# Attention over PSUM in three pairs and a bank: other places for the scores and the row maxima from step 112 on

## The chip, the cores and the metric

The kernel runs on one core of one Trainium2 chip. The metric is the device time of one execution in microseconds (us); three runs were made. The core has five engines that work side by side, each in the order of its own instructions: TensorE (PE, with its weight loads shown apart as PEld), VectorE (DVE), ScalarE (ACT), GpSimd (POOL) and SyncE (SP). Matmul results land in PSUM, which this kernel divides into eight banks of 512 fp32 per partition.

## The reference

A transformer block with modulation from a conditioning vector: layer norm, attention with 16 heads of width 28 over 2048 tokens, then layer norms and an MLP. Dimensions: S = 2048, D = 448, F = 1792.

```python
mod = (silu(c) @ w_mod).reshape(1, 6, 1, D)          # sa, ca, ga, sb, cb, gb
h = layernorm(x) * (1 + ca) + sa
q, k, v = split_heads(h @ wqkv)                      # 16 heads of 28
p = softmax((q @ k.T) * 28 ** -0.5)                  # 2048 x 2048 for each head
x = x + ga * ((p @ v) @ wo)
h = layernorm(x) * (1 + cb) + sb
x = x + gb * (gelu(layernorm(h) @ w1 + b1) @ w2 + b2)
```

## The kernel before

Three phases follow each other. Phase 1 (to 182 us) makes q, k and v, phase 2 (182 to 846 us) is the attention, phase 3 (to the end) the MLP. The order of each engine's instructions is the order in which the Python code issues them; nothing reorders them. Between engines semaphores are set, and they follow from tiles: an instruction waits until the earlier instructions that read or write its tile, or the tile that had the same place, are done.

Heads are taken in four groups `g` of four, queries in four blocks `qt` of 512. A pair (g, qt) is a unit `u` (0 to 15), and a unit has 16 steps `kt`, one for each 128 keys, so phase 2 has 256 steps. In step s of unit u PE computes the transposed scores of 128 keys and 512 queries for the four heads. Each head has 32 rows of the array, so up to four of its matmuls run side by side. The scores come in two halves (`hf`): heads 0 and 1, then heads 2 and 3. A half is a tile of two banks made by six matmuls (three terms of a split product, two heads). ACT takes the exponential of a half in one instruction (128 x 1024), and four matmuls, later called the AV block, multiply the exponentials of the step before with v into the bank `o`. They use all 128 rows and 32 columns each.

The softmax needs its row maximum. It is computed for later units in advance: `max_one` makes a block of scores with queries along partitions (one matmul on 32 rows, 512 keys) in a bank, and DVE reduces the bank to one column. Such a matmul with its reduction is called a maximum here. The queue `mxq` holds them, `emit_max(n, half)` issues the next ones, for heads of the asked half where it finds one, and `finish_max` issues what is still missing for a unit six steps before it starts. The tables `plain`, `left_steps` and `n_maxima` give each step its number: four and three by turns in ordinary steps.

Units 11 to 15 end with an output product. Four steps of the following unit (`kt` 8 to 11, told by `is_wo`) run `t_wo` after their AV block: nine matmuls of 128 x 448 for the block of unit 11, twelve for units 12 to 14, accumulated in one bank by `mm_acc`. ACT copies it out and POOL adds it to x. Before, such a step issues from none to three maxima.

PSUM in phase 2 is `o` with one bank, three banks with the tag `mx` (maxima and output products by turns), and two tiles `s` of two banks for score halves. Once all maxima are issued, `share(1, 3)` changes this to one `mx` bank and three `s` tiles.

Of the kernel before, what the change touches and what calls it, by code (L numbers as in the profile page):

```python
# [13 lines left out]
F32 = mybir.dt.float32  # L14
F32R = mybir.dt.float32r
AF = mybir.ActivationFunctionType
# [6 lines left out]
D = 448  # L23
# [18 lines left out]
def tile_adaln_block(ctx: ExitStack, tc: tile.TileContext, x, wqkv, wo, w1, b1, w2, b2, c, w_mod, out):  # L42
# [13 lines left out]
    def nm(t):  # L56
        uid[0] += 1
        return f"{t}_{uid[0]}"
# [253 lines left out]
    kh_sb = {}  # L312
    qh_sb = {}

    def mm_acc(p, terms):
        for i, (a, b) in enumerate(terms):
            pe.matmul(p, a, b, start=(i == 0), stop=(i == len(terms) - 1))  # L317

# [168 lines left out]

    last_j = [None]  # L490

    def emit_max(n, half=None):
        for _ in range(n):
            if not mxq:
                return
            fits = [x for x, m in enumerate(mxq[:32]) if half is None or (m[4] // 2 == half and m[4] != last_j[0])]
            g, qt, cch, i, j = mxq.pop(fits[0] if fits else 0)
            last_j[0] = j
            max_one(g, qt, cch, i, j)
            count(g, qt, [cch])  # L500


# [256 lines left out]
    def unit_end_tasks(u, o_sb):  # L759
        g, qt = divmod(u, NB)  # L760
        st = {}
        staged = g < last_g(qt)
        parts = [g] if g > last_g(qt) else list(range(g + 1))

        def t_den():
            q_ = pool if u >= NU - 2 else sp
            den = sbt("den", [128, 16], bufs=2)
            q_.dma_start(den, o_sb[DH:128:32, :].rearrange("j (q r) -> j q r", r=16))
            st["den"] = den

        def t_rec():
            q_ = pool if u >= NU - 2 else sp
            rec = st["den"]
            dve.reciprocal(rec, rec)
            drec = dr.tile([4, 512], F32, tag="drec", name=nm("drec"), bufs=2)
            q_.dma_start(drec.rearrange("j (q r) -> (j q) r", r=16), rec)
            rb = sbt("osb", [128, 512], bufs=2)
            q_.dma_start(rb, drec[:, None, :].broadcast_to([4, 32, 512]))
            st["rb"] = rb

        def t_split():
            st["on"] = st["rb"]
# [206 lines left out]
    pend = None  # L989
    o = None  # L990
    plain = [0]
    three = False


    def is_wo(s_):
        return s_ // NKT >= NU - NB and 8 <= s_ % NKT < 12


    def left_steps(s_):
        rest = range(s_, NKT * (NU - 1) - 6)  # L1000
        n_wo = sum(is_wo(x) for x in rest)
        return len(rest) - n_wo, sum(is_wo(x) and x % NKT > 8 for x in rest)


    def n_maxima(s_):
        n_plain, n_wo = left_steps(s_)
        over = len(mxq) - 7 * n_plain // 2
        if is_wo(s_):
            return max(0, -(-over // max(n_wo, 1))) if s_ % NKT > 8 else 0
        plain[0] += 1  # L1010
        return 4 if plain[0] % 2 or (over > 3 * n_wo and over > 0) else 3

    def av(u, kt, p, o):
        g = u // NB
# [10 lines left out]
        return slot(("c0", "c1", "d0")[p_no[0] % 3], [128, 4, 512], F32)  # L1025

    p_next = p_tile()
    done_max = set()
    for u in range(NU):
        g, qt = divmod(u, NB)  # L1030
        for kt in range(NKT):
            step = u * NKT + kt
            if kt == 1 and u + 1 < NU and u + 1 not in qst:
                load_q(u + 1)
            if kt == NKT - 6 and u + 1 < NU:
# [6 lines left out]
            n = n_maxima(step)  # L1042
            n0 = 1 if n == 3 and step % 4 == 3 else 2

            ks, qs = kst[(g, kt // 4)], qst[u]
            kc = slice((kt % 4) * 128, (kt % 4 + 1) * 128)
            for hf in range(2):
                s2 = ps_s2()
                for term, (kp, qp) in enumerate(((0, 0), (1, 0), (0, 1))):
                    for jj in range(2):  # L1050
                        rows_ = slice(64 * hf + 32 * jj, 64 * hf + 32 * jj + 32)
                        pe.matmul(s2[:, jj, :], ks[rows_, kp, kc], qs[rows_, qp, :], start=(term == 0), stop=(term == 2))  # L1052
                    if hf == 0 and term < min(n0, n):
                        emit_max(1, 1)
                    if hf == 1 and ((term == 0 and n - n0 > 0) or (term == 2 and n - n0 > 1)):
                        emit_max(1, 0)
                if hf == 1:
                    p_next = p_tile()
                    pt.append(p_next[:, 0:2, :])
                act.activation(pt[hf], s2, AF.Exp, scale=SCALE)  # L1060
            if pend is not None:
                pu, pkt, pp, po = pend
                av(pu, pkt, pp, po)
# [99 lines left out]
```

## Time and profile before

| | |
|---|---|
| median of 3 runs | 1146.88 us (1146.44 to 1147.62) |
| profiled execution | 1144.6 us, its span 1142.7 us |
| mean granted TensorE clock | 0.999 |
| PE, DVE, ACT busy | 1130.1, 827.9, 683.4 us |
| phase 2 | 182 to 846 us |
| first exponential of step 112 | at 460.7 us |

The profiled execution takes 1.9 us more than its span, which runs from the first to the last instruction. It is 2.3 us below the median of the runs. Busy time is a union of recorded instructions. Matmuls are pipelined, and several on different rows of the array overlap, so PE busy all the time says that something is in flight, not that its array is full. In groups, "x" is the count, the number after the bar the busy time in us, then the mean ns of one, then the idle time of the engine before it and what ended it. In tables by stretch, a column gives the busy time in the stretch and the count of instructions.

### The profile page before, as it was taken

What the parts mean: (1) busy time and instruction counts of PE and PEld (TensorE: products, weight loads), DVE (VectorE), ACT (ScalarE), POOL (GpSimd) and SP (SyncE); (2) the same over time, 40 slices, a digit from 0 to 9 for tenths busy, and PEclk for the clock granted to TensorE, in tenths of its full rate; (3) what the DMA queues carried; (4) which work ended last, traced back from release to release, by engine and by line L of the source; (5) the groups of instructions that cost most, each with busy time, mean ns of one, the idle gap of its engine ahead of it and who ended that gap; (6) DMA issues with size and microseconds to landing.
All of it is one profiled execution on the core that took longest, in us unless ns stands there. A gap on an engine that the chain in (4) does not pass through costs nothing.

```text
span 1142.7 us, 20811 instructions
## 1 busy us (share of the span) xinstructions
PE 1130.1 (99%) x8380; PEld 678.2 (59%) x8380; DVE 827.9 (72%) x1487; ACT 683.4 (60%) x839; POOL 217.0 (19%) x235
## 2 busy tenths in 40 slices
PE   8999999999999999999999999999999999999998
PEld 6767765444444444444444444545458888888887
DVE  6868787999997899989999977483648853444322
ACT  4656757878876887878888777676862321211110
POOL 2533432210000000000000011204514503123000
PEclk9999999999999999999999999999999999999999
DMA  9642354111131111321110222022213100000000
GB/s 300 205 147 108 112 175 140 43 61 57 51 97 59 58 39 38 95 66 58 57 57 22 85 83 72 15 84 77 60 55 87 42 34 1 1 33 1 33 1 33
DMA packets 51305, 81.09 MB, mean 71 GB/s; under 512 B 12700, under 2 KB 21760, under 8 KB 51208
## 3 DMA queue, kind: packets, MB, share of 16 engines
q1 hardware_dynamic: 50248, 78.73, 21.8%
q8 instruction: 66, 1.08, 0.4%
q0 software_dynamic: 672, 0.56, 0.2%
q10 hardware_dynamic: 288, 0.46, 0.1%
q14 instruction: 31, 0.25, 0.1%
HBM read 53.11 MB, written 26.35 MB: 70 GB/s over the span
## 4 chain that ended last, share of the span: by engine, by line
PE 92%; DVE 2%; DMA 2%; ACT 1%; POOL 1%; issue 1%; SPq 0%; DVEq 0%; ACTq 0%; POOLq 0%
PE s L1052 25%; PE o L1016 21%; PE mx L317 16%; PE pa L339 7%; PE mx L392 7%; PE s L1113 4%; PE s L1114 4%; PE s L1112 4%; PE pa L317 3%; PE o L240 1%; DMA slot_c<-in_w_mod_dram 1%; PE mx L240 1%; DMA den<-osb 1%; POOL xn L849 0%; POOL xn L848 0%
## 5 line engine op out<-in xcount | busy, mean ns | idle before, releaser
L397 DVE TENSOR_REDUCE mxp<-mx 128x1 f32<-128x512 f32 x919 | 579.3, 684 | 101.5 <-PE mx L392 95.7
L1060 ACT ACTIVATE slot_c<-s 128x1024 f32<-128x1024 f32 x341 | 339.6, 1022 | 82.2 <-PE s L1052 81.8
L1052 PE MATMUL s<-slot_b,slot_a 32*128 32x512 f32 x3072 | 377.9, 421 | 1.6 <-ACT full L814 0.7
L1052 PEld LDWEIGHTS s<-slot_b,slot_a 32*128 32x128 f32 x3072 | 212.5, 183 | 250.0 <-ACT slot_c L1060 146.1
L392 PE MATMUL mx<-kh,qh 32*128 32x512 f32 x899 | 292.6, 470 | 1.7 <-DVE mxp L397 1.3
L1016 PE MATMUL o<-slot_c,v 128*32 128x512 f32 x1364 | 271.4, 606 | 0.5 <-ACT osb L984 0.4
L1060 ACT ACTIVATE slot_d<-s 128x1024 f32<-128x1024 f32 x171 | 174.7, 1022 | 38.7 <-PE s L1052 38.0
L1016 PE MATMUL o<-slot_d,v 128*32 128x512 f32 x684 | 180.8, 607 | 0.0
L1096 ACT ACTIVATE full<-mx,b_col 128x512 f32<-128x512 f32 x56 | 38.5, 688 | 191.7 <-PE mx L317 179.6
L392 PEld LDWEIGHTS mx<-kh,qh 32*128 32x128 f32 x899 | 116.4, 182 | 12.8 <-DVE mxp L397 7.6
L1099 DVE CAST hi<-full 128x512 fp32r<-128x512 f32 x56 | 25.2, 450 | 129.2 <-ACT full L1096 129.2
L783 POOL TENSOR_TENSOR osb<-osb,osb 128x512 f32<-128x512 f32 x16 | 21.1, 1319 | 460.1 <-DMA osb<-drec 460.1
L1016 PEld LDWEIGHTS o<-slot_c,v 128*32 128x32 f32 x1364 | 38.1, 108 | 54.9 <-issue 50.1
L317 PE MATMUL mx<-y,slot_a 128*128 128x512 f32 x160 | 60.6, 395 | 0.0
L405 ACT ACTIVATE slot_d<-mx 128x512 f32<-128x512 f32 x48 | 27.0, 597 | 40.0 <-PE mx L392 39.8
L1100 DVE TENSOR_TENSOR lo<-full,hi 128x512 fp32r<-128x512 f32 x56 | 44.1, 788 | 5.2
L317 PE MATMUL mx<-y,slot_c 128*128 128x512 f32 x152 | 47.5, 396 | 0.1
L1114 PE MATMUL s<-slot_v,lo 128*128 128x448 f32 x128 | 46.7, 365 | 0.0
L1112 PE MATMUL s<-slot_v,hi 128*128 128x448 f32 x128 | 46.6, 364 | 0.0
L1016 PEld LDWEIGHTS o<-slot_d,v 128*32 128x32 f32 x684 | 24.7, 108 | 27.5 <-issue 25.2
L317 PE MATMUL mx<-y,slot_v 128*128 128x512 f32 x112 | 39.2, 396 | 0.0
L317 PE MATMUL mx<-y,slot_b 128*128 128x512 f32 x112 | 39.0, 397 | 0.0
(223 smaller groups left out, 1411.2 us busy)
## 6 DMA issues: line engine op xcount, KB each, us to landing
d<-lo SPq DMA_DIRECT2D x32, 256.0 KB
slot_b<-d SPq DMA_DIRECT2D x32, 256.0 KB
slot_a<-d SPq DMA_DIRECT2D x32, 256.0 KB
d<-hi SPq DMA_DIRECT2D x20, 256.0 KB
osb<-drec SPq DMA_DIRECT2D x14, 256.0 KB
out_dram<-xn SPq DMA_DIRECT2D x16, 224.0 KB
slot_v<-in_w_mod_dram SPq DMA_DIRECT2D x4, 784.0 KB
raw<-in_B_w_dram SPq DMA_DIRECT2D x14, 224.0 KB
```

The lines of the kernel that those rows point to most:

```text
L317: pe.matmul(p, a, b, start=(i == 0), stop=(i == len(terms) - 1))
L339: pe.matmul(p, *ts[i], start=(i == 0), stop=(i == len(ts) - 1))
L392: pe.matmul(m, qh_sb[(g, qt)][js, i * 128 : (i + 1) * 128], k[js, :], start=True, stop=True)
L397: dve.tensor_reduce(out=mxp[(g, qt)][:, i, j, cch : cch + 1], in_=m, op=ALU.max, axis=AX.X)
L1016: pe.matmul(o[32 * j : 32 * j + 32, :], v_sb[kt // 4][:, kt % 4, 4 * g + j, :], p[j // 2][:, j % 2, :], start=(kt == 0), stop=(kt == NKT - 1),
L1052: pe.matmul(s2[:, jj, :], ks[rows_, kp, kc], qs[rows_, qp, :], start=(term == 0), stop=(term == 2))
L1060: act.activation(pt[hf], s2, AF.Exp, scale=SCALE)
L1096: act.activation(gf, p, AF.Gelu_apprx_tanh, bias=b1_col[:, i : i + 1])
L1100: dve.tensor_tensor(out=glo, in0=gf, in1=f(ghi), op=ALU.subtract)
L1112: pe.matmul(pp, ghi[:, ts], w_hi, start=(m == 0), stop=False)
L1113: pe.matmul(pp, ghi[:, ts], w_lo, start=False, stop=False)
L1114: pe.matmul(pp, glo[:, ts], w_hi, start=False, stop=(m == NFT - 1))
```

## The change

From the first step at which the room suffices for all maxima still to be issued (`room`; this is step 112, the start of unit 7), PSUM is divided into `o`, one bank `mx` and three tiles of two banks, `pair0` to `pair2`. Up to step 111 everything is as before. From there:

- The first score half of a step always goes to the same pair. The second half takes one of the two other pairs, and two maxima take the other; after the step those two pairs change places. A third maximum takes the `mx` bank, between the two halves.
- Each ordinary step issues three maxima. In odd steps the half of heads 2 and 3 comes first.
- In `t_wo`, while maxima are left, the product is accumulated in the first bank of a pair. After its first five matmuls (`i == 5` in `mm_acc`) six maxima are issued: two in each of the other pairs, one in `mx`, one in the product's second bank. Then the product goes on, and the three pairs change their roles by one. So an output step issues nine maxima. In the step behind it all three maxima come after the scores.
- The planned numbers `left_steps` and `n_maxima` go. For the last unit `finish_max` comes four steps ahead instead of six. When the queue is empty, scores go round over all three pairs.

All told 410 maxima stand behind step 112 in both kernels. Units 7 to 11 issue 56 each before and 48 now, unit 12 51 and now 72, unit 13 49 and now 72, unit 14 30 and now 26.

The core of the diff:

```diff
+    def ps_pair(i):
+        return psp[0].tile([128, 2, 512], F32, tag=f"pair{i}", name=nm("pair"), bufs=1)
-    def mm_acc(p, terms):
-        for i, (a, b) in enumerate(terms):
-            pe.matmul(p, a, b, start=(i == 0), stop=(i == len(terms) - 1))
+    def mm_acc(p, terms, done=0, mid=None):
+        for i in range(done, len(terms)):
+            if i == 5 and mid:
+                mid()
+            pe.matmul(p, *terms[i], start=(i == 0), stop=(i == len(terms) - 1))
...
-                p = ps_mx()
+                p, spare = wo_banks()
...
-                mm_acc(p[:, :D], terms)
+                mm_acc(p[:, :D], terms, 0, spare)
...
+    def wo_banks():
+        if not mxq:
+            return ps_mx(), None
+        first, g_, b_ = pairs
+        t = ps_pair(first)
+        pairs[:] = [g_, b_, first]
+
+        def spare():
+            for i in (g_, b_):
+                m = ps_pair(i)
+                for x in range(2):
+                    emit_max(1, x, lambda: m[:, x, :])
+            emit_max(1, 0)
+            emit_max(1, 1, lambda: t[:, 1, :])
+
+        return t[:, 0, :], spare
...
-            if not (three or mxq or late):
-                three = True
-                share(1, 3)
+            if not pairs and room(step):
+                pairs = [0, 1, 2]
+                share(1, 0)
...
-            for hf in range(2):
-                s2 = ps_s2()
+            halves = (1, 0) if pairs and step % 2 else (0, 1)
+            for x, hf in enumerate(halves):
+                s2 = ps_pair(pairs[x]) if pairs else ps_s2()
...
+                if pairs and x == 0 and not (step and is_wo(step - 1)):
+                    emit_max(1, halves[1])
...
+            if mxq and pairs:
+                m = ps_pair(pairs[2])
+                for x in range(2):
+                    emit_max(1, halves[0], lambda: m[:, x, :])
+                if step and is_wo(step - 1):
+                    emit_max(1, halves[1])
+                pairs = [pairs[0], pairs[2], pairs[1]]
+            elif pairs:
+                pairs = [pairs[2], pairs[0], pairs[1]]
```

In the rows below, `s` and `pair` are the tiles of two banks, `mx` the single banks, `o` the AV block's bank. What an instruction waits for stands in brackets: the semaphore of DVE, of ACT (Activation) or of a DMA queue. First PE in an ordinary step with four maxima, before; L1052 is a score, L392 a maximum, L1016 the AV block:

```order
L1052 MATMUL s_5556<-slot_b_1117_4909,slot_a_934_4070 128x512 [waits Activation_49]
L1052 MATMUL s_5556<-slot_b_1117_4909,slot_a_934_4070 128x512
L392 MATMUL mx_5559<-kh_1131_4970,qh_793_3416 128x512 [waits DVE_49]
L1052 MATMUL s_5556<-slot_b_1117_4909,slot_a_934_4070 128x512 x2
L392 MATMUL mx_5564<-kh_1131_4970,qh_793_3416 128x512 [waits DVE_49]
L1052 MATMUL s_5556<-slot_b_1117_4909,slot_a_934_4070 128x512 x2
L1052 MATMUL s_5570<-slot_b_1117_4909,slot_a_934_4070 128x512 [waits Activation_49]
L1052 MATMUL s_5570<-slot_b_1117_4909,slot_a_934_4070 128x512
L392 MATMUL mx_5573<-kh_1131_4970,qh_793_3416 128x512 [waits DVE_49]
L1052 MATMUL s_5570<-slot_b_1117_4909,slot_a_934_4070 128x512 x4
```

Here a maximum has the next of three banks, and its wait is for the reduction of the maximum three places ahead of it. The step's fourth maximum and its AV block follow. Now PE in the second and third step of unit 7 of the changed kernel, from the first step's `mx` maximum to the third step's last maximum; L1069 is a score, L397 a maximum, L1032 the AV block:

```order
L397 MATMUL mx_5957<-kh_1096_4814,qh_859_3729 128x512
L1069 MATMUL pair_5961<-slot_b_1117_4909,slot_a_905_3934 128x512 [waits DVE_49]
L1069 MATMUL pair_5961<-slot_b_1117_4909,slot_a_905_3934 128x512 x5
L397 MATMUL pair_5970<-kh_1096_4814,qh_859_3729 128x512 [waits Activation_49]
L397 MATMUL pair_5970<-kh_1096_4814,qh_859_3729 128x512 [waits DVE_49]
L1032 MATMUL o_5446<-slot_d_1339_5939,v_258 32x512 x2
L1032 MATMUL o_5446<-slot_c_1334_5911,v_258 32x512 x2
L1069 MATMUL pair_5991<-slot_b_1234_5447,slot_a_905_3934 128x512 [waits Activation_49]
L1069 MATMUL pair_5991<-slot_b_1234_5447,slot_a_905_3934 128x512 x5
L397 MATMUL mx_5998<-kh_1096_4814,qh_859_3729 128x512
L1069 MATMUL pair_6002<-slot_b_1234_5447,slot_a_905_3934 128x512 [waits DVE_49]
L1069 MATMUL pair_6002<-slot_b_1234_5447,slot_a_905_3934 128x512 x5
```

The two maxima of a pair stand next to each other, directly ahead of the AV block, and the second has a wait of its own for DVE, as has the first matmul of the second score half. The semaphore counts DVE's finished instructions. The second maximum of `pair_5970` asks for count 678, which the reduction of the first maximum of the same tile brings; the second half in `pair_6002` asks for 679, which the reduction of the second maximum brings.

Last PE in the output product of the second output step of unit 12, before (nine matmuls in a row) and in the changed kernel:

```order
L317 MATMUL mx_9001<-slot_e_514_2139,slot_a2h_8726 128x448 [waits DVE_49]
L317 MATMUL mx_9001<-slot_e_515_2140,slot_a2h_8726 128x448
L317 MATMUL mx_9001<-slot_e_514_2139,slot_a2h_8726 128x448
L317 MATMUL mx_9001<-slot_e_514_2139,slot_a3h_8729 128x448
L317 MATMUL mx_9001<-slot_e_515_2140,slot_a3h_8729 128x448
L317 MATMUL mx_9001<-slot_e_514_2139,slot_a3h_8729 128x448
```

After the rows shown three more of the same kind follow. In the changed kernel (L322 is the product):

```order
L322 MATMUL pair_8796<-slot_e_515_2140,slot_a3h_8523 128x448
L397 MATMUL pair_8802<-kh_1648_7574,qh_1398_6240 128x512 [waits DVE_49] x2
L397 MATMUL pair_8807<-kh_1648_7574,qh_1398_6240 128x512 [waits Activation_49]
L397 MATMUL pair_8807<-kh_1648_7574,qh_1398_6240 128x512 [waits DVE_49]
L397 MATMUL mx_8812<-kh_1648_7574,qh_1398_6240 128x512
L397 MATMUL pair_8796<-kh_1648_7574,qh_1398_6240 128x512
L322 MATMUL pair_8796<-slot_e_514_2139,slot_a3h_8523 128x448 [waits DVE_49]
L322 MATMUL pair_8796<-slot_e_514_2139,hi_8677 128x448
```

The six maxima stand between the product's fifth and sixth matmul. The second one of each pair waits for the reduction of the first, and the sixth matmul of the product waits for the reduction of the last of the six, which lies in the other bank of the product's tile.

More of the change, by code (lines that the diff above doesn't have):

```diff
@@ L490, in tile_adaln_block, with emit_max @@
     last_j = [None]
-    def emit_max(n, half=None):
+    def emit_max(n, half=None, ps=None):
         for _ in range(n):
@@ L498, in emit_max @@
             last_j[0] = j
-            max_one(g, qt, cch, i, j)
+            max_one(g, qt, cch, i, j, ps)
             count(g, qt, [cch])
@@ L991, in tile_adaln_block, with room, finish_step @@
     plain = [0]
-    three = False
+    pairs = []
     def is_wo(s_):
         return s_ // NKT >= NU - NB and 8 <= s_ % NKT < 12
[L999 to L1011, printed above, removed]
+    def room(s_):
+        need = 0
+        for u in range(s_ // NKT, NU):
+            need += left.get(divmod(u, NB), 64)
+            if need > sum(9 if is_wo(x) else 3 for x in range(s_, finish_step(u))):
+                return False
+        return True
+    def finish_step(u):
+        return NKT * u - (4 if u + 1 == NU else 6)
+    def wo_banks():
[12 more added lines that the diff above has]
+        return t[:, 0, :], spare
     def av(u, kt, p, o):
@@ L1027, in tile_adaln_block @@
     p_next = p_tile()
-    done_max = set()
     for u in range(NU):
@@ L1034, in tile_adaln_block @@
                 load_q(u + 1)
-            if kt == NKT - 6 and u + 1 < NU:
+            if u + 1 < NU and step == finish_step(u + 1):
                 finish_max(*divmod(u + 1, NB))
             tick_late()
-            if not (three or mxq or late):
-                three = True
-                share(1, 3)
+            if not pairs and room(step):
+                pairs = [0, 1, 2]
+                share(1, 0)
             pt = [p_next[:, 2:4, :]]
-            n = n_maxima(step)
+            plain[0] += 1
+            n = 4 if plain[0] % 2 else 3
             n0 = 1 if n == 3 and step % 4 == 3 else 2
@@ L1052, in tile_adaln_block @@
                         pe.matmul(s2[:, jj, :], ks[rows_, kp, kc], qs[rows_, qp, :], start=(term == 0), stop=(term == 2))
-                    if hf == 0 and term < min(n0, n):
+                    if not pairs and hf == 0 and term < min(n0, n):
                         emit_max(1, 1)
-                    if hf == 1 and ((term == 0 and n - n0 > 0) or (term == 2 and n - n0 > 1)):
+                    if not pairs and hf == 1 and ((term == 0 and n - n0 > 0) or (term == 2 and n - n0 > 1)):
                         emit_max(1, 0)
-                if hf == 1:
+                if pairs and x == 0 and not (step and is_wo(step - 1)):
+                    emit_max(1, halves[1])
+                if x == 1:
                     p_next = p_tile()
                     pt.append(p_next[:, 0:2, :])
-                act.activation(pt[hf], s2, AF.Exp, scale=SCALE)
+                act.activation(pt[x], s2, AF.Exp, scale=SCALE)
+            if mxq and pairs:
[7 more added lines that the diff above has]
+                pairs = [pairs[2], pairs[0], pairs[1]]
+            pt = [pt[halves[0]], pt[halves[1]]]
             if pend is not None:
```

## The prediction

> **What bounds the kernel now.** I began with the page: its busy times, the chain that ended last and the costliest groups.
>
> ```profile
> span 1142.7 us, 20811 instructions
> PE 1130.1 (99%) x8380; PEld 678.2 (59%) x8380; DVE 827.9 (72%) x1487; ACT 683.4 (60%) x839; POOL 217.0 (19%) x235
> ...
> PE 92%; DVE 2%; DMA 2%; ACT 1%; POOL 1%; issue 1%; SPq 0%; DVEq 0%; ACTq 0%; POOLq 0%
> ...
> L397 DVE TENSOR_REDUCE mxp<-mx 128x1 f32<-128x512 f32 x919 | 579.3, 684 | 101.5 <-PE mx L392 95.7
> L1060 ACT ACTIVATE slot_c<-s 128x1024 f32<-128x1024 f32 x341 | 339.6, 1022 | 82.2 <-PE s L1052 81.8
> ```
>
> PE carries 92% of the chain, while one reduction of a maximum keeps DVE 0.68 us. Next I cut phase 2 at the first exponentials of steps 112, 192, 200 and so on. The table counts the exponentials, two a step (one that reaches over a border counts twice). Its first column is the time of the stretch.
>
> ```profile
> core 0: us, ACT busy (x), PEclk, DMA share, GB/s
> 460.71:657.67 196.96, 155.18 (x160) 1.00 0.21 63
> 657.67:677.38 19.71, 15.51 (x17) 1.00 0.37 115
> 677.38:695.06 17.68, 7.76 (x8) 1.00 0.00 1
> 695.06:724.82 29.76, 23.38 (x25) 1.00 0.26 82
> 724.82:744.70 19.88, 7.76 (x9) 1.00 0.00 1
> 744.70:774.23 29.53, 23.26 (x24) 1.00 0.26 82
> 774.23:802.22 27.99, 15.49 (x17) 1.00 0.27 86
> ```
>
> The first, second, fourth and sixth are 80, 8, 12 and 12 ordinary steps: 196.96 + 19.71 + 29.76 + 29.53 = 275.96 us for 112, or 2.46 each. The third and fifth are four output steps each, 17.68 + 19.88 = 37.56. The last ends with steps that have no maxima left. Third, PE's timeline of one short step, then the pieces around a late maximum of the long step ahead of it, and the first reductions of the short step on DVE.
>
> ```profile
> 605.60 0.50 PE L1052 MATMUL s<-slot_b,slot_a 32*128 32x512 f32 x2
> 605.86 0.72 PE L1052 MATMUL s<-slot_b,slot_a 32*128 32x512 f32 x8
> 606.40 0.39 PE L392 MATMUL mx<-kh,qh 32*128 32x512 f32 x2
> 606.75 1.06 PE L1016 MATMUL o<-slot_c,v 128*32 128x512 f32 x8
> 607.74 0.50 PE L1052 MATMUL s<-slot_b,slot_a 32*128 32x512 f32 x2
> ```
>
> ```profile
> 603.43 0.69 DVE L397 TENSOR_REDUCE mxp<-mx 128x1 f32<-128x512 f32 x1 [0.26 <-PE mx L392]
> 604.18 0.18 PEld L392 LDWEIGHTS mx<-kh,qh 32*128 32x128 f32 x1
> 604.61 0.62 PE L1016 MATMUL o<-slot_d,v 128*32 128x512 f32 x2
> 603.43 2.48 DVE L397 TENSOR_REDUCE mxp<-mx 128x1 f32<-128x512 f32 x4 [0.26 <-PE mx L392]
> 606.18 1.35 DVE L397 TENSOR_REDUCE mxp<-mx 128x1 f32<-128x512 f32 x2 [0.26 <-PE mx L392]
> ```
>
> The short step is 2.14 long (605.60 to 607.74): 1.15 to its AV block, then 0.99. No engine waits long in it, because a maximum finds one of three banks free while DVE reduces the others. The reduction at 603.43 ends at 604.12, the weight load that waited for it starts 0.06 later, and the AV block another 0.43 later. Two reductions back to back take 1.35, so the second adds 0.66 here, and the long step's four (four ended 2.48 after the first began) add 0.60 each.
>
> **An ordinary step after the change.** The second maximum of a pair, B2, may not start until DVE has reduced the first, B1. The order of PE shows the wait. B2 stands ahead of the AV block, so the AV block and the whole next step are queued behind it, and ACT's next exponentials wait for that step's scores. Counted from the step's first score:
>
> - B1 goes to rows that have had three score matmuls, the fourth place of those rows. In the short step the matmuls in this place start at 606.40, and the reduction behind them at 606.18 + 1.35 - 0.69 = 606.84, which is 1.24 after the step's start.
> - The reduction: 0.69. Its end to B2's weight load: 0.06. From there to the AV block: 0.43. AV block to the next step: 0.99.
>
> Sum 1.24 + 0.69 + 0.06 + 0.43 + 0.99 = 3.41; I take 3.40, from the unrounded starts. B2's own reduction starts some 0.55 after its load (load to end 0.49, then 0.06), at 2.54, and ends at 3.23: just ahead of the next step, so the next second half waits little. The `mx` maximum comes early and its reduction is over by 1.24. The exponentials need 2.04 of the 3.40, so ACT has room.
>
> Bounds: 2.14, the short step, if this wait cost nothing, and 4.0, if B1's reduction always came behind another (0.60). No row shows a second maximum waiting on the first of its own tile, but each of the chain's links has a row, so I keep 3.3 to 3.5. For 112 steps: 380.8 - 275.96 = **+104.8 us**.
>
> The other edits in ordinary steps cost nothing: three maxima instead of 3.5 save matmuls that ran beside scores, the swap of halves changes rows alone, and the earlier loads of the groups' keys are under a slower loop. The second score half needs the reductions (3.23, above); if B2's came 0.2 later, that wait would add what it exceeds.
>
> **An output step after the change.** One product of nine matmuls and the two ends of one of twelve:
>
> ```profile
> 682.49 1.06 PE L1016 MATMUL o<-slot_c,v 128*32 128x512 f32 x8
> 683.48 0.87 PE L317 MATMUL mx<-slot_e,slot_a2h 128*128 128x448 f32 x3
> 684.20 0.77 PE L317 MATMUL mx<-slot_e,slot_a3h 128*128 128x448 f32 x3
> 685.22 0.36 PE L317 MATMUL mx<-slot_e,lo 128*128 128x448 f32 x1
> 685.51 0.50 PE L1052 MATMUL s<-slot_b,slot_a 32*128 32x512 f32 x2
> ...
> 829.44 0.87 PE L317 MATMUL mx<-slot_e,slot_a2h 128*128 128x448 f32 x3
> 832.09 0.51 PE L1052 MATMUL s<-slot_b,slot_a 32*128 32x512 f32 x4
> ```
>
> Nine take 2.03 (683.48 to 685.51), twelve 2.65, 0.20 each; from the last one to a matmul on 32 rows it is 0.29. The fifth starts at 684.20 + 0.20, so 0.92 after the first, and the first of the six maxima loads at 0.92 + 0.29 = 1.21. Load to next load over a reduction is 0.49 + 0.06 + 0.69 + 0.06 = 1.30: the second maximum loads at 2.51, the third beside it. Their reductions start at 3.06 and 3.67, the fourth may load at 4.42 with the last two beside it, and the three reductions then start at 4.97, 5.57 and 6.17 and end at 6.86. Only then, at 6.92, does the product go on. The sixth matmul would have come at 1.12, and it pays a change of mode, 0.10 (the first three of a product take 0.87, the next three 0.77): **5.9 us for each of eight output steps**. Its lower bound is 0.8, the two changes of mode and the maxima on PE, its upper one 6.5, with one reduction late.
>
> An output step is then 3.40 + 2.03 + 5.90 = 11.33 with nine matmuls and 3.40 + 2.65 + 5.90 = 11.95 with twelve. Four of each are 93.1, against 37.56: **+55.5 us**. The row at 774.23 I leave as it is: unit 14 loses two maxima in its output steps, which may give 1.5 back.
>
> **The clock.** Before, DVE once left PE idle. The first rows are PE alone by stretches, with its granted clock in the column behind busy time and count; the others are PE's timeline there.
>
> ```profile
> 348.30:351.72 3.42, 2.21 (x16) 1.00 0.04 4
> 351.72:355.13 3.41, 3.41 (x21) 0.50 0.21 77
> 355.13:358.54 3.41, 3.41 (x35) 1.00 0.29 77
> 13.80:17.20 3.40, 2.73 (x20) 1.00 1.04 342
> ...
> 349.68 0.50 PE L392 MATMUL mx<-kh,qh 32*128 32x512 f32 x1 [1.13 <-DVE mxp L397]
> 352.00 1.07 PE L1016 MATMUL o<-slot_d,v 128*32 128x512 f32 x2
> 353.86 0.79 PE L1052 MATMUL s<-slot_b,slot_a 32*128 32x512 f32 x2
> 355.56 0.64 PE L1016 MATMUL o<-slot_c,v 128*32 128x512 f32 x4
> ```
>
> With PE busy for 2.21 of 3.42 us the clock fell to half for the next 3.41; with 2.73 of 3.40 it stayed. The halved stretch took 1.86 for an AV block (0.99) and 1.70 for the scores behind it (1.15): 1.4 more. In the 5.7 us among the six maxima PE has three groups of 0.5 in flight, 26%, so I expect one halved stretch for each, 8 x 1.4 = **+11 us**, between 0 and 20. An ordinary step has 1.19 + 1.42 = 2.61 of 3.40 busy (77%), nearer to the row that kept its clock. The Trainium skill, "TensorE: Matmul & The Clock Gate", section "HAM oscillation — how this bites in real kernels", puts it as a rule that PE gaps up to some 3.4 us are harmless. By it these 11 us would not come, since no gap here is above 2.1; the row at 349.68 speaks against it with a gap of 1.13.
>
> **Sum.** 104.8 + 55.5 + 11 = 171 us. On the profiled execution's 1144.6 that is 1316; the median of the runs stands 2.3 above, so **1318 us**.
>
> **The rivals.**
>
> 1. The waits are there, but the clock stays full: the pieces of idleness in an output step are each short, about 0.8 us twice and 2.1 once. Against it stands 349.68. It gives 1318 - 11 = 1307. (The rule named above says the same.)
> 2. The clock falls in ordinary steps too, as 77% lies between the 65% that lost it and the 80% that kept it. Were every second stretch of 3.41 halved, 381 us would hold 56 of them, at 1.4: +78, so 1396.
> 3. Faster: the two maxima of a pair run side by side, each with its bank, and their waits end early. Then a step's bound is the next second half, which waits for both reductions: 1.24 + 0.60 + 0.69 + 0.06 = 2.59 after the step before began, then 0.92 (1.15 less one of four places) and 0.99, for two steps: 4.50, 2.25 each. 112 steps take 252.0, saving 24.0. Eight output steps are bound by nine reductions of 0.61, 44.0, which costs 6.4. So 1146.9 - 17.6 = 1129. It needs ordinary steps under 2.41. The order of PE speaks against it: the wait's count is that of the pair's own first reduction.
> 4. No change: the waits cost what half a maximum less saves, 2.46 a step and 4.7 an output step. B1 would have to be reduced 0.94 earlier than its place in the rows allows.
>
> **How the numbers follow.** The forecast has 0.76, the first rival 0.11, the second 0.07, the third 0.04, the fourth 0.02. The range should hold the forecast and the first rival: an ordinary step of 3.3 to 3.5 makes -11 to +11, the clock -11 to +9, the output steps -5 to +5. From 1318 that gives 1291 to 1343 if they hardly coincide; I widen the upper end to 1350 for a few halved ordinary steps. Faster by over 0.2% (2.3 us, about what a measurement of this kernel can tell): 0.04, within it 0.01, slower 0.95.
>
> **What would show it.** In the changed kernel's profile the chain should hand some 15% to the reductions. An ordinary step should last 3.4, with about 0.8 of PE idle ahead of the pair's second maximum, released by DVE. Output steps should last 11 to 14, and halved clocks should stand there alone. I am wrong if PE starts the second maximum of a pair beside the first, if the steps lie near 2.3, or if the clock is low throughout.

## The result, and the profile after

The changed kernel takes 1379.43 us (median of four runs, 1375.23 to 1396.16), against 1146.66 for the kernel before beside it: 1.2024 times as long, interval 1.1986 to 1.2062. The longest of the four ran at a lower granted clock (0.949, the others at 0.962 to 0.969) and is left out of the ratio. The profiled execution took 1382.02 us, with a span of 1380.3. The forecast was 1318, in a range of 1290 to 1350: the direction was right, the size 61 us short.

First the page of the changed kernel: the span and busy times, the granted clock in 40 slices, the chain by engine, and the costliest groups of maxima.

```profile
span 1380.3 us, 20815 instructions
PE 1196.4 (87%) x8380; PEld 695.5 (50%) x8380; DVE 841.4 (61%) x1487; ACT 683.5 (50%) x839; POOL 217.0 (16%) x235
...
PEclk9999999999999999999999965987999999999999
...
PE 81%; DVE 15%; DMA 1%; issue 1%; ACT 1%; SPq 0%; DVEq 0%; ACTq 0%
...
L402 DVE TENSOR_REDUCE mxp<-mx 128x1 f32<-128x512 f32 x636 | 409.1, 685 | 190.5 <-PE pair L1069 140.7
L402 DVE TENSOR_REDUCE mxp<-pair 128x1 f32<-128x512 f32 x283 | 193.6, 686 | 136.6 <-PE pair L397 129.2
L397 PE MATMUL pair<-kh,qh 32*128 32x512 f32 x283 | 125.7, 480 | 154.9 <-DVE mxp L402 154.9
```

(L1069 is a score here, L397 a maximum, L402 its reduction, L1032 the AV block, L322 the product, L1079 an exponential.) Two lines show the new wait. PE stood idle for 154.9 us ahead of maxima in pairs, released by DVE; before, all of DVE's part of the chain was 2%. And the reductions of `mx` were released, for 140.7 of their 190.5 us of waiting, by a score matmul and not by a maximum. That second line is the one the forecast lacked, as will be seen.

Next, phase 2 cut at the first exponentials of the same steps as before:

```profile
core 0: us, ACT busy (x), PEclk, DMA share, GB/s
464.09:769.69 305.60, 155.09 (x161) 0.99 0.14 41
769.69:801.35 31.66, 15.51 (x17) 0.96 0.17 55
801.35:861.54 60.19, 7.75 (x8) 0.59 0.00 0
861.54:908.83 47.29, 23.27 (x25) 0.94 0.16 51
908.83:966.38 57.55, 7.75 (x8) 0.73 0.00 1
966.38:1013.11 46.73, 23.27 (x24) 0.96 0.16 52
1013.11:1039.47 26.36, 15.50 (x16) 1.00 0.28 91
```

Against the rows of before, the ordinary stretches (first, second, fourth, sixth) grew from 275.96 to 431.28 us: +155.3. The output steps (third, fifth) grew from 37.56 to 117.74: +80.2, and the clock column shows 0.59 and 0.73 there. The last stretch lost 1.6. Up to the first exponential of step 112 there are 3.4 more (464.09 against 460.71), and behind the last of these stretches 0.3. Together 237.6, the difference of the spans. Of the 3.4, some 2 come from steps 110 and 111, which last 3.25 and 3.82: the new arrangement begins in step 111, one step earlier than the text on the change says. The rest comes from a longer halved stretch in unit 4.

Now one ordinary step, PE and then DVE. The step begins at 601.29 and the next one at 605.10, so it lasts 3.81.

```profile
601.29 0.50 PE L1069 MATMUL pair<-slot_b,slot_a 32*128 32x512 f32 x2
601.31 0.50 PE L397 MATMUL mx<-kh,qh 32*128 32x512 f32 x1
601.31 0.97 PE L1069 MATMUL pair<-slot_b,slot_a 32*128 32x512 f32 x9
602.10 0.39 PE L397 MATMUL pair<-kh,qh 32*128 32x512 f32 x1
603.68 0.50 PE L397 MATMUL pair<-kh,qh 32*128 32x512 f32 x1 [1.17 <-DVE mxp L402]
604.10 0.62 PE L1032 MATMUL o<-slot_d,v 128*32 128x512 f32 x2
605.10 0.50 PE L1069 MATMUL pair<-slot_b,slot_a 32*128 32x512 f32 x2
```

```profile
602.34 0.69 DVE L402 TENSOR_REDUCE mxp<-mx 128x1 f32<-128x512 f32 x1 [1.24 <-PE pair L1069]
602.94 0.68 DVE L402 TENSOR_REDUCE mxp<-pair 128x1 f32<-128x512 f32 x1
604.21 0.69 DVE L402 TENSOR_REDUCE mxp<-pair 128x1 f32<-128x512 f32 x1 [0.59 <-PE pair L397]
```

PE is idle for 1.17 us until the pair's first reduction ends at 603.62, as forecast in kind. But look at the first reduction. The `mx` maximum is recorded from 601.31 to 601.81, and its reduction starts only at 602.34, 1.05 after the step began. The row names a score as what released it. The code issues this maximum behind all six scores of the first half, and DVE waits for a count of PE's finished instructions. The last of those scores is recorded as ending at 602.26, 0.08 ahead of the reduction. So the pair's first reduction, which by the forecast would have started at 1.24, found DVE busy and started at 1.65.

Last, PE around the first output product with six maxima inside, and PE in some stretches with its granted clock.

```profile
804.14 0.88 PE L322 MATMUL pair<-slot_e,slot_a2h 128*128 128x448 f32 x3
804.86 0.57 PE L322 MATMUL pair<-slot_e,slot_a3h 128*128 128x448 f32 x2
805.36 0.49 PE L397 MATMUL pair<-kh,qh 32*128 32x512 f32 x1
806.63 0.49 PE L397 MATMUL pair<-kh,qh 32*128 32x512 f32 x2 [0.78 <-DVE mxp L402]
808.51 0.58 PE L397 MATMUL mx<-kh,qh 32*128 32x512 f32 x1
811.06 0.74 PE L322 MATMUL pair<-slot_e,slot_a3h 128*128 128x448 f32 x1 [1.96 <-DVE mxp L402]
```

```profile
core 0: us, PE busy (x), PEclk, DMA share, GB/s
474.26:477.68 3.42, 2.24 (x23) 1.00 0.04 5
477.68:481.09 3.41, 3.29 (x22) 0.50 0.66 199
522.05:525.46 3.41, 2.23 (x23) 1.00 0.45 126
525.46:528.88 3.42, 2.25 (x23) 1.00 0.53 186
808.77:836.08 27.31, 19.65 (x73) 0.50 0.00 0
839.50:866.81 27.31, 19.64 (x82) 0.50 0.00 1
```

The product's sixth matmul comes 811.06 - 804.14 = 6.92 after its first, which is the figure of the forecast. The clock did more than forecast: it stayed at half for 27.31 us, twice in the output steps of unit 12, and there was one halved stretch at 477.68, far from any output step.

### The profile page after: what moved, and what is told of

The parts are those of the page before. It is cut to its first block, busy times and chain, and to the rows that moved or that the text cites. A ratio compares the mean times of both kernels' runs of the same rounds, so it can differ in the third digit from the quotient of the medians.

```text
span 1380.3 us, 20815 instructions
## 1 busy us (share of the span) xinstructions
PE 1196.4 (87%) x8380; PEld 695.5 (50%) x8380; DVE 841.4 (61%) x1487; ACT 683.5 (50%) x839; POOL 217.0 (16%) x235
## 4 chain that ended last, share of the span: by engine, by line
PE 81%; DVE 15%; DMA 1%; issue 1%; ACT 1%; SPq 0%; DVEq 0%; ACTq 0%
PE o L1032 18%; DVE mxp L402 14%; PE mx L322 12%; PE pair L1069 10%; PE s L1069 9%; PE pa L344 6%; PE pair L397 6%; PE mx L397 4%; PE s L1142 3%; PE s L1143 3%; PE s L1141 3%; PE pa L322 3%; PE pair L322 2%; DMA slot_v<-in_A_wqkv_dram 1%; PE o L243 1%
## 5 line engine op out<-in xcount | busy, mean ns | idle before, releaser
L402 DVE TENSOR_REDUCE mxp<-mx 128x1 f32<-128x512 f32 x636 | 409.1, 685 | 190.5 <-PE pair L1069 140.7
L1032 PE MATMUL o<-slot_c,v 128*32 128x512 f32 x1364 | 277.9, 621 | 0.4 <-ACT osb L989 0.4
L402 DVE TENSOR_REDUCE mxp<-pair 128x1 f32<-128x512 f32 x283 | 193.6, 686 | 136.6 <-PE pair L397 129.2
L1079 ACT ACTIVATE slot_c<-pair 128x1024 f32<-128x1024 f32 x193 | 192.1, 1021 | 142.8 <-PE pair L1069 142.4
L397 PE MATMUL pair<-kh,qh 32*128 32x512 f32 x283 | 125.7, 480 | 154.9 <-DVE mxp L402 154.9
L397 PE MATMUL mx<-kh,qh 32*128 32x512 f32 x616 | 223.1, 483 | 1.4 <-DVE mxp L402 0.9
L1032 PE MATMUL o<-slot_d,v 128*32 128x512 f32 x684 | 184.4, 618 | 1.0 <-ACT slot_d L1079 1.0
L1069 PE MATMUL pair<-slot_b,slot_a 32*128 32x512 f32 x1740 | 178.2, 437 | 0.4 <-DVE mxp L402 0.4
L1069 PE MATMUL s<-slot_b,slot_a 32*128 32x512 f32 x1332 | 169.2, 422 | 0.9 <-ACT v L381 0.6
L1079 ACT ACTIVATE slot_c<-s 128x1024 f32<-128x1024 f32 x148 | 147.3, 1022 | 40.8 <-PE s L1069 40.8
L397 PEld LDWEIGHTS pair<-kh,qh 32*128 32x128 f32 x283 | 51.5, 194 | 222.8 <-DVE mxp L402 215.8
L1069 PEld LDWEIGHTS pair<-slot_b,slot_a 32*128 32x128 f32 x1740 | 103.4, 194 | 119.3 <-ACT slot_c L1079 60.8
L1069 PEld LDWEIGHTS s<-slot_b,slot_a 32*128 32x128 f32 x1332 | 95.2, 184 | 116.0 <-ACT slot_c L1079 70.9
L1079 ACT ACTIVATE slot_d<-pair 128x1024 f32<-128x1024 f32 x97 | 99.1, 1021 | 73.1 <-PE pair L1069 72.7
L397 PEld LDWEIGHTS mx<-kh,qh 32*128 32x128 f32 x616 | 86.5, 185 | 8.2 <-DVE mxp L402 5.6
L1079 ACT ACTIVATE slot_d<-s 128x1024 f32<-128x1024 f32 x74 | 75.6, 1022 | 18.5 <-PE s L1069 18.3
L1032 PEld LDWEIGHTS o<-slot_c,v 128*32 128x32 f32 x1364 | 38.3, 108 | 49.2 <-issue 44.2
L322 PE MATMUL mx<-y,slot_a 128*128 128x512 f32 x160 | 60.6, 395 | 0.0
```

The costliest lines, as they stand in the source:

```text
L322: pe.matmul(p, *terms[i], start=(i == 0), stop=(i == len(terms) - 1))
L397: pe.matmul(m, qh_sb[(g, qt)][js, i * 128 : (i + 1) * 128], k[js, :], start=True, stop=True)
L402: dve.tensor_reduce(out=mxp[(g, qt)][:, i, j, cch : cch + 1], in_=m, op=ALU.max, axis=AX.X)
L1032: pe.matmul(o[32 * j : 32 * j + 32, :], v_sb[kt // 4][:, kt % 4, 4 * g + j, :], p[j // 2][:, j % 2, :], start=(kt == 0), stop=(kt == NKT - 1),
L1079: act.activation(pt[x], s2, AF.Exp, scale=SCALE)
```

## The experiments

The theory after this reading has three parts. The waits inside a pair exist because a pair is one tile, and they cost nearly all of the loss. About 0.4 us of each ordinary step comes from the place of the `mx` maximum, behind six scores. And the output steps cost some 14 us more than forecast (80.2 against 55.5 + 11) because the clock stays low. The rival for the first part is that three maxima a step are too much for DVE or PE in any layout; for the second, that the second maximum's load or the AV block got slower.

**The `mx` maximum earlier.** It goes behind the first two scores of the first half; nothing else changes.

```diff
                     for jj in range(2):
                         ...
+                    if pairs and x == 0 and term == 0 and not (step and is_wo(step - 1)):
+                        emit_max(1, halves[1])
...
-                if pairs and x == 0 and not (step and is_wo(step - 1)):
-                    emit_max(1, halves[1])
```

> Edit: from step 111 the step's maximum in the mx bank is issued after the first term of the first score half instead of after its last. Theory: in the changed kernel this maximum's reduction starts 1.05 us after the step's start, because its matmul counts as done only after the score matmuls issued ahead of it; so the reduction of the pair's first maximum comes behind it at 1.65, and the second maximum of the pair, the AV block and the next step move with it. Issued early, it should be reduced from about 0.57, the pair's first maximum from 1.24, and an ordinary step should fall from 3.80 to 3.40: about 48 us less, 1330. Rival: the reduction is late for another reason (DVE, or the clock); then the step stays at 3.80 and the time near 1379.

Measured: 1334.64 us (1334.25 to 1336.31), ratio 1.1661 (1.1644 to 1.1679), and an ordinary step of 3.44. Its PE rows from one step start to the next, and DVE in between:

```profile
589.57 0.50 PE L1069 MATMUL pair<-slot_b,slot_a 32*128 32x512 f32 x2
591.59 0.50 PE L397 MATMUL pair<-kh,qh 32*128 32x512 f32 x1 [0.81 <-DVE mxp L402]
593.02 0.50 PE L1069 MATMUL pair<-slot_b,slot_a 32*128 32x512 f32 x2
```

```profile
590.13 0.69 DVE L402 TENSOR_REDUCE mxp<-mx 128x1 f32<-128x512 f32 x1 [0.75 <-PE mx L397]
590.85 0.69 DVE L402 TENSOR_REDUCE mxp<-pair 128x1 f32<-128x512 f32 x1
```

The `mx` reduction now starts 0.56 after the step's start, released by its own maximum, and the pair's first one at 1.28. The wait ahead of the second maximum fell from 1.17 to 0.81. This is the step that the forecast had described, and the time lies 17 us above the forecast. The clock was full from 356 us to the output steps, where it fell as in the changed kernel: they last 13.0 to 15.9. Of the 47.8 us between the two profiles 41 lie in the ordinary steps and 6 in the output steps.

**A tile for each bank.** The order of all instructions stays, but a maximum gets a tile of one bank, so that a wait is for that bank alone. A place of two banks is opened anew each step, as one tile or as two.

```diff
+    def ps_bank(i, x):
+        return place[i].tile([128, 512], F32, tag=f"bank{x}", name=nm("bank"), bufs=1)
...
-                m = ps_pair(pairs[2])
+                m = [ps_bank(pairs[2], x) for x in range(2)]
                 for x in range(2):
-                    emit_max(1, halves[0], lambda: m[:, x, :])
+                    emit_max(1, halves[0], lambda: m[x])
```

(The same for the product and the six maxima in `wo_banks`.)

> Edit: the place of a pair is taken either by one tile of two banks (scores) or by two tiles of one bank (two maxima; product and sixth maximum), so that no maximum waits for a reduction in the neighbouring bank; the order of all instructions stays. Theory: the waits inside a pair are what costs. Then an ordinary step is bound by the second score half, which waits for both reductions of the pair before (1.05, 1.66, 2.27 to 2.95, then 0.06, 0.92, 0.99, over two steps): 2.46 instead of 3.80, and an output step by its nine reductions or by PE, 5.5 to 6.5 instead of 14.7. Total 1379 - 162 - 69 = about 1148 (1135 to 1165), with no halved clock. Rival: nine or three maxima and the changes of array mode cost PE or DVE that time themselves; then output steps stay above 9 us and the total above 1190.

Measured: 1164.37 us (1162.37 to 1165.37), ratio 1.0169 (1.0151 to 1.0186). An ordinary step lasts 2.44, output steps 5.5 to 6.9. Two rows of PE, with the two maxima of a pair side by side among the scores of the second half:

```profile
602.38 0.39 PE L414 MATMUL bank<-kh,qh 32*128 32x512 f32 x2
602.40 0.63 PE L1089 MATMUL pair<-slot_b,slot_a 32*128 32x512 f32 x4
```

With the same order and number of maxima, 215 of the 233 us are gone, and outside unit 4 phase 2 has no halved stretch left. So the loss is the waits that a shared tile brings, with the clock that they cost; DVE and PE can carry three maxima a step. It came out 16 us above what I expected, near the end of the expected range, as an output step took up to 6.9, where I had taken 5.5 to 6.5, and some steps were longer.

**Both edits together.**

> Edit: both edits, own tiles and the early maximum. Theory: the three reductions then run from 0.57, 1.24 and 1.85 to 2.53, the next second half may start at 2.59, and an ordinary step takes (2.59 + 0.92 + 0.99) / 2 = 2.25: about 25 us less than with own tiles alone, 1123 (1110 to 1135). Rival: with own tiles DVE is no longer on the path, and the early maximum changes nothing against own tiles alone.

Measured: 1161.83 us (1159.89 to 1163.96), ratio 1.0152 (1.0129 to 1.0175), a miss. The step fell to 2.38 only. PE and DVE in it:

```profile
600.60 0.40 PE L414 MATMUL bank<-kh,qh 32*128 32x512 f32 x2
600.63 0.63 PE L1089 MATMUL pair<-slot_b,slot_a 32*128 32x512 f32 x4
```

```profile
601.33 1.29 DVE L419 TENSOR_REDUCE mxp<-bank 128x1 f32<-128x512 f32 x2 [0.27 <-PE pair L1089]
```

The two maxima are recorded as done by 601.00, and their reductions start at 601.33, 0.07 after the second half's last score (601.26). It is the same delay once more: the code issues the two maxima behind the six scores of the second half, and the next step's second half waits for both reductions.

**Matmuls that nobody reads, in the waits of the output steps.** Nine 128 x 448 matmuls into the `mx` bank between the six maxima, so that PE is never idle for long.

```diff
+            w_ = ps_mx()
...
+                    if x == 0 or i == g_:
+                        for _ in range(3):
+                            pe.matmul(w_[:, :D], wo_p[0][:, 0, 0:128], wo_p[0][:, 1, :], start=True, stop=True)
```

> Edit: in each of the eight output steps with nine maxima, nine extra matmuls of 128 x 448 that nobody reads go to the mx bank, three each behind the first, second and third of the six maxima, where PE waits for reductions anyway. Theory: the output steps lie above 11.3 to 12 plus 0.4 because the clock is halved for 3.4 to 27 us at a time; with the extra matmuls PE is busier in the waits, the halved stretches get fewer, and output steps fall from 14.7 to 12 to 13, the total by 10 to 20 us. Rival: the time is in the chain of reductions alone, and the total stays or grows by up to 10 us.

Measured: 1388.5 us (1384.25 to 1390.42), ratio 1.2124 (1.2096 to 1.2152), slower instead of faster. The eight output steps together fell by only 6 us in the profiles (111.9 against 117.7), although their granted clock rose to 0.85 in both units, from 0.59 and 0.73: 33 us at half clock in place of 81. So either the nine matmuls cost most of what the clock gave back, or part of what these steps lost was not the clock's; this run alone does not tell. And from step 112 on twelve ordinary steps, which the edit does not touch, were lengthened by halved stretches, where the changed kernel had four. What keeps the clock low stays open.

**Another order of the six maxima.** First the one in `mx` and the one in the product's second bank, then the first of each pair, then the second of each, so that no maximum waits for the reduction right ahead of it.

```diff
-            for i in (g_, b_):
...
             emit_max(1, 0)
             emit_max(1, 1, lambda: t[:, 1, :])
+            m = [ps_pair(i) for i in (g_, b_)]
+            for n_ in range(4):
+                emit_max(1, (0, 1, 1, 0)[n_], lambda: m[n_ % 2][:, n_ // 2, :])
```

> Edit: in the changed kernel's output steps only the order of the six maxima among the product's matmuls changes: first the one in the mx bank and the one in the product's second bank, then the first of each pair, then the second of each pair. Theory: PE waits there for a chain of reductions that its order makes, and the product for the last of the six. With this order the first four need no wait, their reductions run from 1.77 to 4.27 after the product's start, the seconds load at 3.7 and 4.3, and the product goes on at about 4.65 instead of 6.92. The eight output steps lose 2.3 us each of waiting and some of their halved clock (21 us in all before): total 1379 - 18 to 30, about 1355. Rival: DVE's nine reductions or the clock alone set the output steps, whatever the order; then the total stays within 6 us of 1379.

Measured: 1369.77 us (1367.64 to 1387.39), ratio 1.1994 (1.1926 to 1.2062). The output steps gained what was expected: 48.1 and 48.7 us for four, against 60.2 and 57.6, so 21 less. Unit 13's first output step ran at full clock and lasted 10.13; with the product going on at 4.65 in place of 6.92, the sum gives 10.09 for it. The total fell by only some 10 (the intervals of the two ratios overlap), since eight ordinary steps, not four, had a halved stretch, in one place for 13.7 us. Where the clock falls in ordinary steps differs from program to program. In the output steps 53 us were at half clock in place of 81.

**A tile for each bank, and all three maxima early.** If the count of finished matmuls is the delay, the pair's two maxima belong ahead of the second half's last two scores.

```diff
+                    if x == 1 and term == 1 and pairs and mxq and not (step and is_wo(step - 1)):
+                        two_max()
+                        took = True
...
```

> Edit: own tiles, the early maximum, and the pair's two maxima issued ahead of the last term of the second score half instead of behind it. Theory: in the kernel with own tiles and the early maximum the reductions of the two begin only when the last score matmul issued ahead of them is done (1.04 after the second half's start), and the next second half waits for both: 1.04 + 0.61 + 0.68 + 0.05 = 2.38, which is its step. Ahead of the last term they should begin at about 0.89: step 2.23, 121 x 0.15 = 18 us less than 1162, so 1143 (1138 to 1150), level with the kernel before. Rival: the step of 2.38 is set by the exponentials or by PE; then the time stays at 1162 or grows, since the two maxima wait for an exponential and would hold up the last term.

Measured: 1154.46 us (1149.32 to 1156.6), ratio 1.0068 (1.0045 to 1.0091). Ordinary steps are 2.26, where 2.23 was expected. But single steps of 3 to 9 us stand some steps behind a unit's start, and the total missed the 1143 expected by 11.

**In addition, the six maxima behind the product's first matmul** (`if i == 1` in place of `i == 5`), so that more of the product covers their reductions.

> Edit: as the kernel with the two maxima ahead of the last term, and in output steps the six maxima come behind the product's first matmul instead of its fifth. Theory: with own tiles an output step of 6.9 us is a loop: the last reduction of the six, the next step's second maximum, its AV block, the product's first matmuls, the six maxima and their six reductions. Four product matmuls of 0.20 fewer in that loop save 0.8 in six to eight output steps, 4 to 6 us less than the kernel it is built on: 1138. Rival: PE is the bound in output steps; then no difference.

Measured: 1145.69 us (1144.23 to 1148.74), ratio 1.0001 (0.9987 to 1.0016): the time of the kernel before. Output steps fell from 6.9 to 6.1, but 1138 was expected. The long steps remained, and DVE's timeline says what they are:

```profile
506.47 0.26 DVE L796 RECIPROCAL den<-den 128x16 f32<-128x16 f32 x1 [2.20 <-DMA den<-osb]
...
771.29 0.43 DVE L815 CAST hi<-osb 128x512 fp32r<-128x512 f32 x1 [2.98 <-POOL osb L805]
```

The end of a unit takes a reciprocal and a cast on DVE, at fixed steps behind it, with DMA transfers ahead of them. The steps have become shorter and the transfers have not (from the first transfer's issue to this reciprocal it is 1.96 us, here and in the kernel before). So DVE stands still, PE behind it, and the clock falls to half at 509.5 and 772.3. In the kernel before DVE waits there too, for 1.67 and 1.38, and the clock stays full.

**The unit's end later.** The reciprocal and the split behind it come one step later where the result is only stored. The loads of earlier groups' outputs come two steps later, so that they no longer stand ahead of the reciprocal's transfers.

```diff
-        tasks = [(0, t_den), (1, t_rec), (4, t_split), (5, t_split2)]
+        r = 2 if staged else 1
+        tasks = [(0, t_den), (r, t_rec), (r + 3, t_split), (r + 4, t_split2)]
         if len(parts) > 1 and not staged:
-            tasks.append((0, lambda: load_o(qt)))
+            tasks.append((2, lambda: load_o(qt)))
```

> The own_mid1 order, with a unit's reciprocal one step later where its result is only stored, and the three loads of earlier groups' outputs two steps later where an output product follows. Theory: the program before is still ahead of own_mid1 only because DVE, in program order, stops at the reciprocal (2.20 us idle at 506.5) and at the split's cast (2.98 us idle at 771.3) until a transfer has landed, and PE then idles and drops to half clock. Without these stops unit 8 gains 3.5 us, unit 14 4.2, unit 13 1.4 and unit 4 3.4: about 1133 us (1130 to 1141). Rival: the transfers land as late as before and the stop only moves to the next step: 1143 to 1148.

> The kernel before with the same two shifts and nothing else, as a control: only unit 4 has such a stop there (the halved clock at 351.7), worth about 3.4 us, so 1141 to 1144 us. If it falls as far as the other kernel, the shifts and not the new places of the maxima make the gain.

Measured: 1134.26 us (1132.44 to 1134.42), ratio 0.9902 (0.9887 to 0.9918), where 1133 was expected. The control, the kernel before with these shifts alone, took 1141.52 (1140.46 to 1142.75), ratio 0.9971 (0.9960 to 0.9983). So of the 10.6 us gained, 3.4 belong to the shifts alone, and 7.3 come only with the new places of the maxima. DVE's wait of 2.20 is now 0.40, and no stretch of phase 2 is halved:

```profile
503.18 0.25 DVE L796 RECIPROCAL den<-den 128x16 f32<-128x16 f32 x1 [0.40 <-DMA den<-osb]
```

```profile
590.86 0.50 PE L414 MATMUL mx<-kh,qh 32*128 32x512 f32 x1
591.15 0.73 PE L1097 MATMUL pair<-slot_b,slot_a 32*128 32x512 f32 x8
591.66 0.40 PE L414 MATMUL bank<-kh,qh 32*128 32x512 f32 x2
592.04 1.07 PE L1050 MATMUL o<-slot_c,v 128*32 128x512 f32 x8
593.04 0.50 PE L1097 MATMUL pair<-slot_b,slot_a 32*128 32x512 f32 x2
```

```profile
core 0: us, ACT busy (x), PEclk, DMA share, GB/s
457.50:640.30 182.80, 155.51 (x161) 1.00 0.23 68
640.30:744.30 104.00, 62.13 (x65) 1.00 0.16 47
```

The 80 steps from 457.50 take 182.8 us, against 196.96 before. Units 12 and 13, with the output steps, take 104.00, against 47.17 + 49.63 = 96.8 before. So the 80 steps save 14.2 with 40 maxima fewer, and the two units lose 7.2 with 44 more: once the waits are gone, the move pays. (The earlier places have a part in both numbers, so they are no price of a maximum.) This kernel is faster than both others.

## Why the prediction was right in direction and wrong in size

**Right.** The wait of the second maximum on its own pair's reduction, ahead of the AV block, is what makes the kernel slower: chain 15% DVE, PE idle of 154.9 us there, and 215 us gone with a tile for each bank. The links were sized well: reduction to load 0.05 (0.06 in the forecast), load to AV block 0.43 (0.43), AV block to next step 1.00 (0.99). The six maxima inside a product cost what was worked out, 6.92 from its first matmul until it goes on. Unit 14's last row fell by 1.6 (1.5).

**The step that failed: "B1 goes to rows that have had three score matmuls, ... 1.24 after the step's start", with "the `mx` maximum comes early and its reduction is over by 1.24".** The term 1.24 was 1.65, because the `mx` reduction could start only at 1.05, not soon after its own maximum, and ended at 1.74. I had read the maximum's place on the array's rows and not its place in PE's order, though the order quoted in the text on the change shows it behind the first half's scores. The forecast named the case as its upper bound, "4.0, if B1's reduction always came behind another", and dismissed it with that sentence. 112 steps at 0.40 make 45 us of the 61. Moving that one maximum gave steps of 3.44 and 45 us back (1379.43 - 1334.64). The changed kernel itself has a step without this delay: behind unit 13's last output step the `mx` maximum comes after all scores, and that step lasts 3.39, with the wait that was forecast:

```profile
967.35 0.49 PE L397 MATMUL pair<-kh,qh 32*128 32x512 f32 x1 [0.78 <-DVE mxp L402]
```

**The second term: the clock, +11.** It assumed one halved stretch of 3.41 for each output step. In the profile of the changed kernel the output steps took 117.7. The sum for them is 93.1 at full clock, and 0.41 more in the first of each four (behind an output step no `mx` reduction stands ahead of the pair's), so 93.9. So some 24 us are left for the clock, above the upper end of 0 to 20. The number of stretches was what failed: 81 us of these steps were at half clock, some 24 stretches and not eight, as the stretch after a halved one is often halved too (27.3 us in a row is eight). Each cost about 1.0 and not 1.4. That this remainder is the clock's is an inference, but it goes with the time at half clock: 1.8 and 1.9 in two steps with 6.83 at half, 4.6 in two that were at half throughout (15.91). Four more ordinary steps were lengthened (5.05, 5.01, 5.43, 5.24), about 5 us.

**The rest:** the entry at steps 110 and 111 costs some 2, which the forecast left out. The profiled execution lies 66 above its forecast of 1316: 45 from the ordinary step, 14 from the output steps, 5 from halved ordinary steps, some 4 outside these rows, less the 1.6 of unit 14.

**The rivals.** The first (full clock) is wrong. In the ordinary steps around 474.26 PE has no gap above 1.2, and the clock fell behind them. The Trainium skill, "TensorE: Matmul & The Clock Gate", section "HAM oscillation — how this bites in real kernels", has as a rule "no PE-idle gaps >~3.4µs." This case's traces don't agree with it, if it is read as a limit below which gaps do no harm. The second (the clock falls in ordinary steps too) had a grain of truth: 5 us of the 78 it gave. The third (pairs side by side, faster) did not happen, as the order of PE said. When the tiles were split so that it did happen, the step was 2.44 and not 2.25, since the same delay by program order was missing from its sum too. The fourth asked for a pair reduced 0.94 earlier; it came 0.41 later.

## What to carry to other kernels

Place an instruction by its position in its engine's order before its position on the array: here its reader was released only when everything issued ahead of it was done, so a matmul whose result another engine waits for goes ahead of matmuls that nobody waits for yet. Give each bank with its own reader a tile of its own, or a second writer will wait for the first one's reader. When steps become shorter, look at work scheduled a fixed number of steps after a transfer: that transfer has lost time too.

## What the runs showed of the hardware

A maximum recorded as ended at 601.81 released its reader at 602.34, 0.08 after the end of the last score issued ahead of it (602.26), although it ran on other rows of the array and its record starts earlier. The semaphore that both count on was raised at 602.28 and then at 602.31, so the maximum's own count came late. In the runs with the earlier maxima the release moved with the place in the order. The Trainium skill, page "PSUM — Partial Sum Buffer", section "Engine vs sequencer instructions", says that matmuls start and complete in program order. The releases agree with the second half of this. The recorded starts do not show the first half: this maximum's record begins 0.55 before that of the score issued just ahead of it (601.31 against 601.86). Whether the array really finishes in order, or only the count is held back, no run here tells apart.

The share of time in which PE has something in flight does not decide the clock alone. The stretch at 474.26 (2.24 busy of 3.42) was followed by half clock, the one at 522.05 (2.23 of 3.41) was not, in steps of the same kind. Ordinary steps with a gap of 1.17 lost the clock now and then, in four to twelve steps from step 112 on, by kernel; those of 3.44 with a gap of 0.81 kept it until the output steps.
